# A linear-attention layer feeding a soft mixture of experts: the transfer of w behind the table load, the first k and r in halves, and idle products before the last expert

## The chip, the cores and the metric

The kernel runs on one core of one Trainium2 chip. The metric is the device time of one execution in microseconds. Five engines work side by side and wait for each other through semaphores: TensorE (PE in the profile; its weight loads are PEld), VectorE (DVE), ScalarE (ACT), GpSimd (POOL) and SyncE (SP), which here only issues transfers. The transfers themselves run on the core's 16 DMA engines.

## The reference

Two layers follow each other. The first is a recurrent attention over four batches, eight heads, 768 steps and a head size of 48:

```
for t in range(S):
    cur = u * k[t] (outer) v[t]
    y[t] = r[t] @ (state + cur)
    state = w[:, None] * state + k[t] (outer) v[t]
```

The second takes the 3072 by 384 result as x and mixes it softly into 32 slots, four for each of eight experts:

```
logits = x @ phi                       # 3072 x 32
d = softmax of logits over the rows;   slots = d.T @ x
out_e = relu(slots_e @ w1[e]) @ w2[e]  # w1: 384 x 1024, w2: 1024 x 384
c = softmax of logits over the slots;  result = c @ out
```

All inputs are float32. The sixteen expert matrices are by far the most of them.

## The kernel before

**Attention** is done in chunks of 128 steps, two chunks at a time, so that there are 12 units. For each, k and r are scaled by tables of powers of w (`tabs`, `tabl`), turned by TensorE, multiplied into a masked matrix and applied to v; a state runs from unit to unit. **The mixture** follows unit by unit: logits, the two softmaxes, the sums over the rows. When all rows are in, the experts run: H00 to H11 multiply the slots by w1, Q00 to Q13 multiply the hidden values by w2, and 24 products with `LexpT` (line 949) spread the result over the rows, are copied out of PSUM by ScalarE and VectorE in turn (lines 951 and 953) and are stored in eight transfers by SyncE (line 955).

**The order** is written out by hand. The string `ORDER` (lines 9 to 31) names every step, and `_Plan.run` (line 60) records the steps in that order, so that it is the program order on each engine. A step `Lk0` is the load of the first k; `Sk0` scales it on VectorE (line 427), `Tk0` turns it on TensorE. Words with F are idle products: `F19a_4` is four units of 256 columns, two of them to a product, of `mix` with the identity into a PSUM bank that nobody reads (line 861; the letter a names the bank `Ab`).

**The start** stands ahead of the plan, from line 208 on. ScalarE issues the transfer of w (line 211), broadcast over 128 partitions, and then loads its table of functions (line 212); it copies two permutations (lines 255 and 260), takes the logarithm of w (line 283), and from VectorE's products (line 281) it makes `tabs` (lines 287 and 288) and later `tabl` (line 397). TensorE meanwhile multiplies ones (line 219, `keep_warm`). SyncE's queue begins with k0, r0, u, v0, k1, r1. `load_f` (line 192) loads 32 rows of eight heads for one such step: 128 partitions, each holding two pieces (e = 0 and 1, the even and the odd heads) of 1536 bytes for the short steps (m even) and 3072 bytes for the long ones.

**The expert matrices** W0 to W15 are issued by GpSimd (lines 783 and 785), cast to bfloat16 on the way, into buffers that the attention has given back. The last one comes in two transfers: `W15a` holds seven of its eight rows of blocks, `W15` the eighth. Q12 (line 921) multiplies those seven, Q13 the eighth. Before Q12 stand Q11, which needs W14, and before that F19a_4.

Of the kernel before, what the change touches and what calls it, by code (L numbers as in the profile page):

```python
# [26 lines left out]
NB1 L3 AL2 ET2 YE11 AC1 ZT2 RM3 EE2 ZC3 EX3 SU2 F10a_3 X111 X110 XE111:ACT AL3 F11a_1 ET3 W15a ND1 XE110 EE3:ACT LB4  # L27
RM4 DP2 G1 DP3 AC2 EX4 G2 ET4 AL4 G3 G5 LC2 GS EE4 F12_3 DP4 AC3 ZT3 AC4 LX1 NM2 NB2 F13a_1 MG UN SU3 LC3 F14_6 H00
R00:DVE NM3 H01 R01 F15a_5 HT00 ND2 W15 HT01 HE00 F16a_1 Q00 HE01 Q01 H11 LE1:ACT R11 H10 LX2 R10:DVE NB3 LT4 ND3:ACT
SU4 F18a_2 HT11 HT10 HE10 HE11:ACT LC4 NM4 NB4 ND4:DVE Q10 LE2 LX3 LX4 LE3 F19a_4 Q11 Q12 LE4:ACT Q13  # L30
"""


# [12 lines left out]
class _Plan:  # L46
# [7 lines left out]
    def buf(self, pool):  # L54
        return _Buf(pool)

    def add(self, name, engs, fn, deps=(), bufs=()):
        self.by[name] = _Task(name, engs, fn, list(deps), list(bufs))
# [23 lines left out]
def kernel(  # L82
# [13 lines left out]
    B, H, S, D = r.shape  # L96
# [11 lines left out]
    R = 8  # L108
# [5 lines left out]
    CC = NS // U3  # L114
# [11 lines left out]
    def O(ins):  # L126
        return tc.keep_in_program_order(ins)

    pe, dve, act, pool, sp = nc.tensor, nc.vector, nc.scalar, nc.gpsimd, nc.sync
# [5 lines left out]
    RW = 2 * J * D  # L135
# [53 lines left out]

    def load_f(dst, a, m):
        b, lg = divmod(m, 2)
        jn = J if lg else JH
        O(sp.dma_start(out=dst[:, 0:2 * jn * D].rearrange("p (e x) -> p e x", e=2),  # L195
                       in_=a[b].rearrange("h (y j) d -> y h (j d)", j=jn)[lg * CC * R:lg * CC * R + 32]))

# [10 lines left out]
    for t in wu_t:  # L208
        O(dve.memset(t[:], 1.0))

    O(act.dma_start(out=w_f, in_=w.rearrange("(o q e) d -> o q (e d)", o=1, e=2).to_broadcast([C // nQ, nQ, P2])))
    O(act.preload_act_table_set("natural_log_exp_and_others"))

    warm = LexpT[:, 0:512]
    O(dve.memset(warm, 0.0))
# [128 lines left out]
    def consts_d():  # L344
# [5 lines left out]
    L = _Plan(dict(raw=raw, ks=ks_t, vj=vj_t, kn=kn_t, vn=vn_t, AT=AT_t, prs=pr_t[0:1], prl=pr_t[1:2], dv=dv_t,  # L350
                   **{f"{x}T": t for x, t in turned.items()},
                   S=S_t, Z=Z_t, x=x_t, zc=zc_t, Lc=Lc_t, Lcl=[Lc_t[0][:, NS - 2:]], Lsl=[Ls_t[0][:, NS - 2:]], Ls=Ls_t, E=E_t, ET=ET_t, T=T_t, A=[Ab], Y=[Yb], M=[Mb], **{f"xT{j}": [t] for j, t in enumerate(xT_t)}))
    buf, add = L.buf, L.add
# [17 lines left out]
    for m in range(NLD):  # L371
        for i, nm in enumerate("krv"):

            b, o = (kr["k", m][0], RH) if nm == "r" and m % 2 == 0 else (buf("raw"), 0)
            kr[nm, m] = b, o
            add(f"L{nm}{m}", "SP", (lambda b, o, a, m: lambda t: load_f(b.inst[:, o:RW], a, m))(b, o, (k, r, v)[i], m), bufs=[b])

    def load_phi(t):
        O(sp.dma_start(out=phi_f, in_=moe_phi.rearrange("(p q) s -> p q s", q=nM)))
# [13 lines left out]
    for h, av_, x in (("a", argl, slice(0, JH + 1)), ("b", argm, slice(JH, J + 1))):  # L393
        add(f"AH{h}", "DVE", (lambda av_, x: lambda t: argv_part(av_, e17l[:, x]))(av_, x))
        for i in range(2):

            add(f"TB{i}{h}", "ACT", (lambda i, h, av_: lambda t: O(act.activation(  # L397
                out=tabl[i][:, :, JH:J] if h == "b" else tabl[i][:, :, 0:JH],
                in_=av_[:, :, 1 - i:JH + 1 - i], func=AF.Exp, scale=(-1.0, 1.0)[i])))(i, h, av_),
# [3 lines left out]
    for m in range(NLD):  # L403
        lg = m % 2
        pb = TT["p", m] = buf("pr" + "sl"[lg])
        for nm in "krv":
            dstT = TT[nm, m] = buf(nm + "sl"[lg] + "T")
            P = P2 if nm == "v" else 128
            for h in range(1 + lg):
# [11 lines left out]
                else:  # L421
                    i = "kr".index(nm)
# [42 lines left out]
    for n in range(NU):  # L465
# [4 lines left out]
        m = 2 * bt + (ui > 0)  # L470
# [50 lines left out]
        def f_su(t, Mf=Mf, kn=kn, vn=vn, Sold=Sold, pb=pb, n=n, NK=NK):  # L521
# [13 lines left out]
            bufs=[Mf, vn, pb_, kn] + ([Sold] if ui else []))  # L535
# [26 lines left out]
        def f_y(t, Yf=Yf, rT=rT, vn=vn, dvb=dvb, Sold=Sold, Smid=Smid, a=tuple(ATb), n=n):  # L562
# [18 lines left out]
            bufs=[Yf, rTb, vn, dvb, Smid, ATb[0], ATb[1]] + ([Sold] if ui else []))  # L581
# [213 lines left out]
    for n in range(2 * E):  # L795
        wat[n] = buf("raw")
        wat[n].left += 4
        bufs, deps = [wat[n]], []
# [6 lines left out]
    nm = nm_t[(NPC - 1) % 2]  # L805
# [14 lines left out]
        bufs=[SXb])  # L820
# [118 lines left out]
    i = 0  # L939
# [46 lines left out]
```

## Time and profile before

| what | us |
|---|---|
| time, median of 3 runs (lowest, highest) | 119.17 (118.89, 119.31) |
| the profiled execution's own time | 120.24 |
| its span, first to last instruction | 118.5 |
| outside the span | 1.7 |
| busy: PE, DVE, ACT, POOL | 98.0, 94.8, 86.6, 61.0 |
| mean granted TensorE clock | 0.962 |
| moved by DMA | 31.81 MB as written, 39.42 MB read from HBM |

The profiled execution is 1.07 us longer than the median of the runs, so differences are worked out within the profile and then taken from the median. In the timeline each line gives the start in us, the busy time, the engine, the line of the code, what is written from what is read, the count, and in brackets how long the engine had been idle and who ended that. In the table of windows each row gives the stretch, its length, each engine's busy time with the number of instructions, then the granted TensorE clock, the busy share of the 16 DMA engines and the GB/s that they wrote. A share a little over 1 comes from counting whole packets where they begin.

### The profile page before, as it was taken

How to read it: one execution, taken by the hardware profiler on the slowest of the kernel's cores; microseconds unless marked ns; L12 is line 12 of the kernel's file. 1: busy time of each engine (PE TensorE's matmuls, PEld its weight loads, DVE VectorE, ACT ScalarE, POOL GpSimd, SP SyncE). 2: the span in 40 equal slices, each digit the busy share in tenths (PEclk: the TensorE clock that was granted, in tenths of full speed). 3: DMA queues.
4: the chain of work that ended last, by engine and by line, in shares of the span. 5: the costliest groups of instructions: out<-in, count | busy, mean ns of one | idle time of the engine just before them, and what ended most of it. 6: DMA issues, size and time to landing. Idle time of an engine off the chain costs nothing.

```text
span 118.5 us, 3926 instructions
## 1 busy us (share of the span) xinstructions
PE 98.0 (83%) x1660; PEld 71.1 (60%) x1660; DVE 94.8 (80%) x180; ACT 86.6 (73%) x140; POOL 61.0 (52%) x79
## 2 busy tenths in 40 slices
PE   3997895999999999989999989999899985498000
PEld 0364674787888787867788878686453542254000
DVE  6899987898999999999999989999786274099100
ACT  5769894999999999989899799979644151269000
POOL 7605899999999989999999010002303000000000
PEclk9999999999999999999999999999999999869955
DMA  2999999999999999999999999999999995059994
GB/s 31 333 387 374 364 408 397 383 390 401 384 384 391 297 229 223 219 215 214 217 212 221 210 223 207 223 207 219 212 212 218 216 207 104 12 199 407 419 402 166
DMA packets 10441, 31.81 MB, mean 268 GB/s; under 512 B 1080, under 2 KB 4408, under 8 KB 10424
## 3 DMA queue, kind: packets, MB, share of 16 engines
q0 software_dynamic: 2448, 12.58, 51.8%
q1 hardware_dynamic: 7832, 18.93, 42.3%
q8 instruction: 13, 0.21, 0.7%
q10 hardware_dynamic: 144, 0.05, 0.2%
q14 instruction: 4, 0.03, 0.1%
HBM read 39.42 MB, written 4.72 MB: 373 GB/s over the span
## 4 chain that ended last, share of the span: by engine, by line
PE 32%; DMA 23%; POOL 15%; DVE 9%; ACT 6%; issue 4%; SPq 3%; DVEq 0%; ACTq 0%; POOLq 0%
DMA raw<-in_moe_w_dram 16%; POOL mix L427 12%; PE T L436 7%; DMA raw<-in_r_dram 7%; PE Ab L506 3%; DVE mix L953 2%; PE Yb L572 2%; SPq L195 2%; PE T L491 2%; PE Yb L567 2%; DVE AT_all L511 2%; ACT xT_all L359 2%; PE Yb L578 2%; PE T L481 2%; PE T L595 2%
## 5 line engine op out<-in xcount | busy, mean ns | idle before, releaser
L427 POOL TENSOR_TENSOR mix<-raw,tabl 128x768 bf16<-128x768 f32 x15 | 27.7, 1858 | 5.8 <-ACT tabl L397 5.4
L511 DVE TENSOR_TENSOR AT_all<-Ab,mask 128x1024 bf16<-128x1024 f32 x24 | 29.3, 1219 | 1.1 <-PE Ab L506 0.5
L359 ACT COPY mix<-T 128x1024 bf16<-128x1024 bf16 x19 | 19.1, 1021 | 3.9 <-PE T L436 2.3
L436 PEld LDWEIGHTS <-mix 128*128 128x128 bf16 x192 | 11.8, 99 | 2.3 <-DVE mix L427 0.7
L555 DVE TENSOR_TENSOR dv<-vn,Mb 128x768 bf16<-128x768 bf16 x12 | 11.4, 946 | 1.4 <-PE Mb L545 1.1
L427 POOL TENSOR_TENSOR mix<-raw,tabs 128x768 bf16<-128x768 f32 x6 | 10.8, 1815 | 0.0
L359 ACT COPY vT_all<-T 96x1024 bf16<-96x1024 bf16 x10 | 10.2, 1021 | 0.5 <-PE T L436 0.4
L506 PE MATMUL Ab<-mix 64*128 64x128 bf16 x192 | 9.5, 218 | 1.2 <-ACT mix L359 1.0
L359 ACT COPY xT_all<-T 128x768 bf16<-128x768 bf16 (+1 forms) x12 | 9.3, 784 | 1.3 <-PE T L595 1.3
L359 ACT CAST x<-Yb 128x768 bf16<-128x768 f32 x12 | 9.7, 808 | 0.0
L436 PE MATMUL T<-turnl,mix 128*128 128x128 bf16 x128 | 9.6, 219 | 0.1
L359 ACT COPY vn<-T 128x768 bf16<-128x768 bf16 x11 | 8.8, 814 | 0.0
L452 DVE TENSOR_TENSOR pr<-T,mix 128x1024 bf16<-128x1024 bf16 x12 | 8.0, 681 | 0.0
L712 POOL TENSOR_TENSOR Lc<-Ls,sm 128x192 bf16<-128x192 f32 x2 | 1.0, 516 | 13.5 <-ACT E L690 13.5
L506 PEld LDWEIGHTS <-mix 64*128 64x128 bf16 x192 | 5.8, 94 | 3.5 <-issue 0.7
L572 PEld LDWEIGHTS <-AT_all 128*128 128x128 bf16 x192 | 6.6, 96 | 1.6
L359 ACT COPY kn<-T 128x768 bf16<-128x768 bf16 (+1 forms) x10 | 7.2, 722 | 0.1
L418 POOL CAST vj<-raw 128x768 bf16<-128x768 f32 x8 | 6.7, 832 | 0.6 <-POOL phi_s L336 0.6
L436 PEld LDWEIGHTS <-vj 128*96 128x96 bf16 x96 | 6.2, 123 | 1.2 <-issue 0.2
L572 PE MATMUL Yb<-vn,AT_all 128*128 128x48 bf16 x192 | 6.8, 183 | 0.0
L539 DVE TENSOR_TENSOR Z<-Mb,wT 128x384 bf16<-128x384 f32 x12 | 6.6, 553 | 0.1
L481 PE MATMUL T<-ident,mix 128*128 128x128 bf16 x80 | 6.1, 219 | 0.2
(187 smaller groups left out, 237.8 us busy)
## 6 DMA issues: line engine op xcount, KB each, us to landing
raw<-in_moe_w_dram POOLq DMA_DIRECT2D x13, 768.0 KB, 14.4
raw<-in_k_dram SPq DMA_DIRECT2D x4, 768.0 KB, 12.2
raw<-in_r_dram SPq DMA_DIRECT2D x4, 768.0 KB, 12.2
raw<-in_v_dram SPq DMA_DIRECT2D x4, 768.0 KB, 12.2
out_dram<-mix SPq DMA_DIRECT2D x3, 768.0 KB, 4.6
raw<-in_k_dram SPq DMA_DIRECT2D x4, 384.0 KB, 10.9
raw<-in_r_dram SPq DMA_DIRECT2D x4, 384.0 KB, 10.6
raw<-in_v_dram SPq DMA_DIRECT2D x4, 384.0 KB, 10.8
```

The costliest lines, as they stand in the source:

```text
L195: O(sp.dma_start(out=dst[:, 0:2 * jn * D].rearrange("p (e x) -> p e x", e=2), in_=a[b].rearrange("h (y j) d -> y h (j d)", j=jn)[lg * CC * ...
L359: O(act.copy(dst, src))
L418: O(act.copy(o, i_) if t.eng == "ACT" else pool.tensor_copy(o, i_))
L427: O(eng.tensor_mul(src.inst.rearrange("p (j e s) -> p e j s", j=JH, e=2)[:, :, :, 0:D], rv(), tab))
L436: O(pe.transpose(Tb.inst[0:P, jj * 128:(jj + 1) * 128], sv[:, jj, :], (turn, turnl)[lg][:]))
L452: O(dve.tensor_mul(cv(pb), tv(), cv(kT)))
L481: O(pe.transpose(Tb.inst[:, x * 128:(x + 1) * 128], kT.inst[:, x, :], ident[:]))
L506: O(pe.matmul(Abf.inst[:, e, x * C:(x + 1) * C], kT.inst[s, g * nQ + x, :], rT.inst[s, g * nQ + x, :]))
L511: O(dve.tensor_mul(AT.inst[:], Abf.inst[:].rearrange("p e (g t) -> p e g t", g=nQ), mask[:, None, None, :].to_broadcast([128, 2, nQ, C])))
L539: O(dve.tensor_mul(Smid.inst[:], Mf.inst[:, 0:SW].rearrange("p (q d) -> p q d", q=nQ)[:, :, None, :].to_broadcast([128, nQ, 2, D]), wT[:, ...
L555: O(dve.tensor_mul(dvb.inst[:].rearrange("p g e d -> p (g e) d"), vn.inst[:].rearrange("p g e d -> p (g e) d"), Mf.inst[:, 448:448 + 2 * P ...
L572: O(pe.matmul(y[:, x // nQ, q * P2 + e * D:q * P2 + (e + 1) * D], a[x // nQ].inst[:, e, q, :], vn.inst[:, x, e, :], start=False, stop=(c = ...
```

## The change

Three edits. The table load of ScalarE is recorded ahead of the transfer of w, on the same engine. The loads of k0 and r0 become two transfers each, one for each e, which fill the same bytes; SyncE's queue so has two more transfers. And F20a_10, five products of 512 columns into the bank `Ab`, is put between Q11 and Q12. Nothing that is computed changes.

```
-... F19a_4 Q11 Q12 LE4:ACT Q13
+... F19a_4 Q11 F20a_10 Q12 LE4:ACT Q13

-    def load_f(dst, a, m):
+    def load_f(dst, a, m, halves=False):
         b, lg = divmod(m, 2)
         jn = J if lg else JH
+        if halves:
+            for e in range(2):
+                O(sp.dma_start(out=dst[:, e * jn * D:(e + 1) * jn * D],
+                               in_=a[b].rearrange("(q e) (y j) d -> e y q (j d)", e=2, j=jn)[e, lg * CC * R:lg * CC * R + 32]))
+            return

+    O(act.preload_act_table_set("natural_log_exp_and_others"))
     O(act.dma_start(out=w_f, in_=w.rearrange("(o q e) d -> o q (e d)", o=1, e=2).to_broadcast([C // nQ, nQ, P2])))
-    O(act.preload_act_table_set("natural_log_exp_and_others"))

-            add(f"L{nm}{m}", "SP", (lambda b, o, a, m: lambda t: load_f(b.inst[:, o:RW], a, m))(b, o, (k, r, v)[i], m), bufs=[b])
+            add(f"L{nm}{m}", "SP", (lambda b, o, a, m, hv: lambda t: load_f(b.inst[:, o:RW], a, m, hv))(b, o, (k, r, v)[i], m, m == 0 and i < 2), bufs=[b])
```

More of the change, by code (lines that the diff above doesn't have):

```diff
@@ L29 @@
 R00:DVE NM3 H01 R01 F15a_5 HT00 ND2 W15 HT01 HE00 F16a_1 Q00 HE01 Q01 H11 LE1:ACT R11 H10 LX2 R10:DVE NB3 LT4 ND3:ACT
-SU4 F18a_2 HT11 HT10 HE10 HE11:ACT LC4 NM4 NB4 ND4:DVE Q10 LE2 LX3 LX4 LE3 F19a_4 Q11 Q12 LE4:ACT Q13
+SU4 F18a_2 HT11 HT10 HE10 HE11:ACT LC4 NM4 NB4 ND4:DVE Q10 LE2 LX3 LX4 LE3 F19a_4 Q11 F20a_10 Q12 LE4:ACT Q13
 """
```

## The prediction

> **What bounds the kernel now.** I read the page's rows of slices, then the chain that ended last, then the timeline and narrow windows of the two ends.
>
> ```profile
> DMA  2999999999999999999999999999999995059994
> ```
>
> Each digit is 1/40 of the span (2.96 us). The DMA engines are full from the second slice to the 33rd, and again over the stores. So the time is: start of the DMA stream, its volume, the gap in slices 34 to 36, the stores. The chain names the end of the stream:
>
> ```profile
> 82.73 18.82 DMA raw<-in_moe_w_dram
> ...
> 101.60 0.51 PE Yb L921 x7
> ```
>
> W15a is issued at 82.73 and lands at 101.56; TensorE's last seven rows start on it. These 18.8 us are a queue: a full expert matrix writes 786 KB, which at the 215 GB/s of the stretch 60 to 90 takes 3.66 us, so five lay ahead of it. What engines do between 12 and 98 us is therefore covered, as long as the queue doesn't run dry. The two ends are left. First the front:
>
> ```profile
> 0.73 0.63 ACTq L211 DMA_DIRECT2D LexpT<-in_w_dram  x1
> 0.73 0.71 SPq L195 DMA_DIRECT2D raw<-in_k_dram  x1
> ...
> 1.39 1.28 ACT L212 ACT_TABLE_LOAD   x1 [1.39 <-PEq L970]
> ...
> 1.49 0.80 SPq L195 DMA_DIRECT2D raw<-in_r_dram  x1
> ...
> 2.91 0.60 SPq L195 DMA_DIRECT2D raw<-in_v_dram  x1
> ...
> 3.43 0.28 ACT L283 ACTIVATE LexpT<-LexpT 128x96 f32<-128x96 f32 x1
> ```
>
> ```profile
> 2.00:2.50 0.50, 0.48 (x2) 0.00 (x0) 0.47 (x3) 0.50 (x1) 0.43 (x3) 1.00 0.65 78
> 2.50:3.00 0.50, 0.00 (x0) 0.00 (x0) 0.50 (x4) 0.49 (x2) 0.50 (x5) 1.00 0.62 116
> 3.00:3.50 0.50, 0.34 (x3) 0.26 (x4) 0.50 (x4) 0.50 (x4) 0.50 (x4) 1.00 0.89 273
> 3.50:4.00 0.50, 0.50 (x4) 0.22 (x3) 0.27 (x2) 0.21 (x2) 0.50 (x1) 1.00 1.06 393
> ```
>
> No byte moves before 2 us, and the engines are full only from 3.5. Then the back:
>
> ```profile
> 98.91 0.51 PE L921 MATMUL Yb<-tabl,AT_all 128*32 128x384 bf16 x8
> 101.60 0.84 PE L921 MATMUL Yb<-raw,AT_all 128*32 128x384 bf16 x8 [2.17 <-DMA raw<-in_moe_w_dram]
> ```
>
> ```profile
> 102.00:102.50 0.50, 0.43 (x4) 0.14 (x1) 0.00 (x0) 0.03 (x1) 0.00 (x0) 1.00 0.00 0
> 102.50:103.00 0.50, 0.00 (x0) 0.01 (x1) 0.00 (x0) 0.45 (x1) 0.00 (x0) 0.60 0.00 0
> 103.00:103.50 0.50, 0.50 (x3) 0.44 (x3) 0.00 (x0) 0.14 (x1) 0.00 (x0) 0.50 0.12 33
> ...
> 106.00:106.50 0.50, 0.50 (x5) 0.38 (x4) 0.50 (x2) 0.42 (x2) 0.00 (x0) 0.98 1.06 406
> 106.50:107.00 0.50, 0.50 (x5) 0.46 (x4) 0.50 (x2) 0.50 (x3) 0.00 (x0) 1.00 0.74 292
> ```
>
> TensorE waits 2.17 us for W15a, computes 0.84, waits 0.57 for the copy `so`, and about 3.2 us after it ran out of work the granted clock halves, from 102.6 to 106.0. In that time the 24 output products run 0.32 us apart (starts 103.59, 103.91, 104.23); at full clock they run 0.16 apart (106.74, 106.90, 107.06). The first stores are fed by the slow ones: the DMA share climbs only to 0.83 in the window 105 to 106 and dips to 0.74 at 106.5.
>
> **Part 1, idle products (F20a_10).** Five products of 512 columns; line 861 does two in 0.49 us at full clock (82.92), so 5 x 0.22 = 1.1 us. They start behind Q11 at 99.42 and end at 100.5: beside the wait, 1.07 us before W15a lands. Their bank is next written by an output product, later on the same engine, so nobody waits for them. In the 3.4 us up to 102.60 TensorE was busy about 0.23 + 0.84 = 1.07 us (31%) and the clock fell; with 1.1 more it is 64%. The threshold isn't in the trace: 31% loses the clock, stretches of 85% and more keep it. I take it that 64% keeps it, from the side on which most of the stretch is work.
>
> What that is worth, by the third store (three row groups, issued 105.83). At full clock the products come 0.16 apart, and the copies become the limit: VectorE's start 0.47 apart in warm stretches (108.16, 108.62, 109.09). First copy of VectorE at 103.39 (now 103.52), its second 103.69, then 104.16 and 104.63, which ends at 105.18; the third store goes out at 105.27 instead of 105.83. The dip at 106.5 shows that the DMA engines were waiting for just this store, and afterwards they are full to the end, so its 0.56 us go straight to the end: **-0.55 us**, at most -0.65; 0 if the clock falls all the same.
>
> The Trainium skill, "TensorE: Matmul & The Clock Gate", section "Why this matters for your kernels", asks for no idle gap over about 3 us and puts the drop after one idle window. That speaks against this edit: the largest gap here is 2.17 us, so by that sentence the clock would hold without the products and the term would be 0. The trace differs (0.50 from 102.6 to 106.0), and the measurement decides; the 3.4 us of the dip agree with its window.
>
> **Part 2, halves.** Two more issues on SP. A half has 128 rows. The nearest rows: stores of 128 rows take 0.33 to 0.36 us on SP, the issue of w's 128 rows 0.63 on ACT, loads of 256 rows 0.60 undisturbed. Ends 0.33 and 0.63; I take 0.45, nearer to SP's own rows. With the 0.05 between issues and u's 0.53, v0 goes out at 0.73 + 4 x 0.50 + 0.58 = 3.31 instead of 2.91 (2.83 to 4.03 at the ends), and all issues behind it as much later, until the queue is full: from 8.73 on single issues last up to 2.5 us because they wait for room.
> First bytes: w's came 0.8 us after the end of its issue (2.16), k0's 0.96 after (2.40). A first half issued by 1.18 then moves at about 2.1, 0.3 us sooner than k0 does now. Does v0 come in time? k0 and r0 are 393 KB each, 1.04 us at 378 GB/s. Started 0.3 sooner they end near 4.7; v0, 1.6 us behind its issue, arrives at 4.9 (4.4 to 5.6). So the gain of 0.3 is kept on an engine that is behind the others, and lost by 0.2 on one that is ahead; and the end is set by the engine that is last (shares fall 0.81, 0.45, 0.25, 0.08 from 98 to 102, so most had long finished). I take **-0.2 us**, bounds -0.4 and +0.6.
>
> **Part 3, w behind the table.** Either ScalarE's sequencer sends the table load off and issues w at once (about 0.8), or it issues after the load, at 2.0. The only row is the other order: there the load began at 1.39, 0.03 us behind the issue, so an issue does hold the load up. Bounds for w's landing: +0.05 and +1.28 us over 3.43. Between them I take the first for the sum, as a transfer needs nothing of ScalarE's datapath. Its price is the same, though: 0, as long as the cover holds. With the late w, line 283 moves 1.28, the tables too; GpSimd's first product (10.33, waiting for ScalarE's line 397) starts at 11.61 and ends at 13.45, where now the second starts at 12.48, on r1's landing: +0.97 for everything behind it. The expert issues move too, but lie up to 18.8 us deep in the queue; the first has least room (issued 35.55, its bytes flow from 38.7, the loads ahead drain near 40.5). Q11 would end at 100.4, the idle products at 101.5, just under the landing of W15a.
> The Trainium skill, "Perfetto Trace Analysis", section "DVE / Act Engine Instruction", has the sequencer free again once an instruction is pushed to a wait queue, and in "DMA Instruction — HWDGE" the sequencer itself issues transfers: by it w would not be late. No run here shows that order yet.
>
> **Sum**: -0.55 - 0.2 + 0 = -0.75 us: 120.24 becomes 119.5 under the profiler, 119.17 becomes **118.4** (0.63% faster).
>
> **Rivals.**
> - *The clock falls all the same* (64% is not enough, or the products lie in the wrong stretch). For it: one stretch is all we see. Then only the front counts: 119.0.
> - *v0 starves the DMA engines*: issues of 0.63 us. For it: the issues of w, k0 and r0 all take 0.63 or more. The front costs +0.6 instead of -0.2: 119.2 with the clock held, 119.8 without. Against: SP's 128-row stores.
> - *Slower: late tables push the idle products onto the path.* w issued at 2.0 and landing as late as k0 does (4.1 us later instead of 2.7) comes 2.7 us late. GpSimd then loses 13.03 + 1.84 - 12.48 = 2.4; Q11 ends at 101.8, and the products delay Q12 to 102.9, 1.3 us behind the landing. Less 0.55 for the clock: 119.9. It begins at 1.07 us of delay, and outweighs the gains above from about 1.8.
>
> **How the numbers follow.** Forecast 0.56 (118.4, alone 118.0 to 118.8), clock falls 0.16 (119.0), starved 0.14 (119.2, a third of it 119.8), late tables 0.14 (119.9). About 0.3% (0.36 us) is what a measurement can tell from no change: faster means under 118.81, slower over 119.53. So faster 0.56, same 0.26 (clock falls, two thirds of starved), slower 0.18. Range 118.0 to 119.7: it leaves out the worst of the last two.
>
> **What would show it.** Right: granted clock 1.00 through 102 to 109 and output products 0.16 apart from the first; third store 0.5 us sooner behind `so`; SP's first issue under 0.5 us and first bytes near 2.1; the landing of W15a near 101.3; line 283 at about 3.5. Wrong: a clock of 0.5 behind the idle products; a share under 0.9 near 4.5 to 5.5; line 283 beyond 4.5, with [idle] before Q12 gone.

## The result and the profile after

The changed kernel takes **120.30 us** (median of 20 runs, 119.50 to 120.98); the kernel before took 119.53 us beside it (median of 20, 118.86 to 121.16). The ratio is 1.0066, 95% interval 1.0043 to 1.0090: **slower by 0.66%**, some 0.8 us. The forecast was 118.4 us and faster, so it had the wrong sign. The two profiled executions hide this, because the one of before (120.24 us, span 118.5) lay high among its runs and the one of after (119.82, span 118.0) low. Spans are therefore not compared below, only stretches inside them. Ratios leave out executions that ran slower as a whole, so a ratio can stand a little off that of the medians, and e6 and e16, whose profiled execution was of that kind, have no rates in the table of runs.

**The middle is as it was.** First the row of DMA shares on the page of after, a digit to 1/40 of the span, then the links of its chain that end the stream:

```profile
DMA  2899999999999999999999999999999998149994
```

```profile
83.43 18.39 DMA raw<-in_moe_w_dram
101.82 0.04 issue
101.86 0.83 PE Yb L927 x8
```

The engines are full from the second or third slice to the 33rd, and W15a again spends 18.4 us in the queue. Whatever volume is missing at the front is therefore paid near 101.86. It moved the wrong way: Q12 starts 0.26 later than before (101.60), where the forecast had it 0.3 sooner.

**The front** on SyncE's queue, from the timeline of after (start, busy time, engine, line):

```profile
0.73 1.27 SPq L198 DMA_DIRECT2D raw<-in_k_dram  x2
2.05 1.24 SPq L198 DMA_DIRECT2D raw<-in_r_dram  x2
3.33 0.53 SPq L387 DMA_DIRECT2D LexpT<-in_u_dram  x1
3.92 0.62 SPq L201 DMA_DIRECT2D raw<-in_v_dram  x1
```

A half costs 0.58 to 0.63 us to issue (the first two lines hold two each, with some 0.05 between them), as much as a whole transfer of 256 rows (v0, the last line, 0.62). So v0 goes out at 3.92 instead of 2.91. The windows of after, to be laid beside those of before in the prediction (the last three columns are granted clock, DMA share and GB/s):

```profile
2.00:2.50 0.50, 0.50 (x2) 0.00 (x1) 0.47 (x4) 0.49 (x3) 0.43 (x3) 1.00 0.53 58
2.50:3.00 0.50, 0.30 (x3) 0.30 (x4) 0.50 (x5) 0.35 (x2) 0.50 (x5) 1.00 0.90 316
3.00:3.50 0.50, 0.50 (x4) 0.23 (x3) 0.28 (x2) 0.00 (x0) 0.50 (x4) 1.00 1.12 350
3.50:4.00 0.50, 0.50 (x3) 0.22 (x2) 0.00 (x0) 0.19 (x1) 0.50 (x1) 1.00 1.04 234
4.00:4.50 0.50, 0.50 (x3) 0.15 (x1) 0.37 (x1) 0.09 (x1) 0.50 (x2) 1.00 0.83 184
...
5.50:6.00 0.50, 0.24 (x2) 0.00 (x0) 0.38 (x3) 0.50 (x2) 0.00 (x0) 1.00 0.50 111
```

In the last of these stretches before had the first row below; the second is its row for 5 to 8 us, and the one by itself that of after:

```profile
5.50:6.00 0.50, 0.50 (x2) 0.15 (x1) 0.50 (x1) 0.50 (x1) 0.00 (x0) 1.00 0.98 335
...
5.00:8.00 3.00, 3.00 (x22) 1.64 (x21) 2.89 (x6) 1.93 (x4) 0.00 (x0) 1.00 1.03 368
```

```profile
5.00:8.00 3.00, 1.85 (x17) 0.90 (x16) 2.85 (x7) 2.18 (x5) 0.00 (x0) 1.00 0.82 267
```

Three things are to be read here. The stream does start sooner (316 GB/s from 2.5 to 3, where before had 116). Then, at 3.5, the engines are occupied (share 1.04) but move only 234 GB/s where before moved 393: their packets of 1536 bytes take longer (0.11 us on the mean from 3.5 to 4.5, before 0.07). And by 5.5 to 6 half of their time is idle, share 0.50. Added up over stretches against before: 2 to 3.5 us +0.13 MB (242 against 156 GB/s), 3.5 to 5 us -0.20 MB (250 against 382), 5 to 8 us -0.30 MB (267 against 368). In the first 16 us after moves 4.63 MB, before 4.90. At the 390 GB/s that both reach later, the missing 0.27 MB are 0.7 us. In these two executions only 0.26 us of that are left where W15a lands.

**ScalarE** in after:

```profile
0.73 1.28 ACT L217 ACT_TABLE_LOAD   x1 [0.73 <-PEq L976]
0.76 0.65 ACTq L218 DMA_DIRECT2D LexpT<-in_w_dram  x1
...
3.81 0.28 ACT L289 ACTIVATE LexpT<-LexpT 128x96 f32<-128x96 f32 x1 [0.96 <-DMA LexpT<-in_w_dram]
```

w is issued at 0.76, beneath the table load that began at 0.73. That w lands 0.38 later than before comes from the halves, which now move ahead of it: with the same order on ScalarE and whole transfers (run e3_w), line 283 starts at 3.43 as before, and with the halves and the old order (run e1_halves) it starts at 4.04. From e3_w:

```profile
3.43 0.28 ACT L283 ACTIVATE LexpT<-LexpT 128x96 f32<-128x96 f32 x1 [0.58 <-DMA LexpT<-in_w_dram]
```

**The back** of after: TensorE, then windows, then SyncE's third store, and by itself that of before.

```profile
99.61 0.51 PE L927 MATMUL Yb<-tabl,AT_all 128*32 128x384 bf16 x8
100.05 1.25 PE L867 MATMUL Ab<-mix,ident 128*128 128x512 bf16 x5
101.86 0.81 PE L927 MATMUL Yb<-raw,AT_all 128*32 128x384 bf16 x8 [0.56 <-DMA raw<-in_moe_w_dram]
...
103.57 0.33 PE L955 MATMUL Mb<-so,LexpT 128*128 128x384 bf16 x1
103.73 0.33 PE L955 MATMUL Ab<-so,LexpT 128*128 128x384 bf16 x1
```

```profile
102.50:103.00 0.50, 0.18 (x1) 0.15 (x1) 0.00 (x0) 0.28 (x1) 0.00 (x0) 1.00 0.00 0
...
106.50:107.00 0.50, 0.50 (x4) 0.33 (x3) 0.50 (x2) 0.50 (x2) 0.00 (x0) 1.00 0.98 406
```

```profile
105.51 3.41 SPq L961 DMA_DIRECT2D out_dram<-mix  x4
```

```profile
105.83 3.61 SPq L955 DMA_DIRECT2D out_dram<-mix  x4
```

The granted clock stays at 1.00, output products start 0.16 apart, the third store goes out at 105.51 (105.83 before, although Q12 started 0.26 later), and the dip to 0.74 at 106.5 has become 0.98. In this execution the part did what was forecast.

### The profile page after: what moved, and what is told of

It reads as the page before. It is cut to its first block, busy times and chain, and to the rows that moved or that the text cites. A ratio compares the mean times of both kernels' runs of the same rounds, so it can differ in the third digit from the quotient of the medians.

```text
span 118.0 us, 3934 instructions
## 1 busy us (share of the span) xinstructions
PE 97.9 (83%) x1661; PEld 71.1 (60%) x1665; DVE 94.1 (80%) x180; ACT 86.9 (74%) x140; POOL 61.4 (52%) x79
## 4 chain that ended last, share of the span: by engine, by line
PE 37%; DMA 18%; ACT 14%; DVE 14%; issue 4%; POOL 4%; DVEq 0%; ACTq 0%; POOLq 0%
DMA raw<-in_moe_w_dram 16%; PE T L442 9%; PE Ab L512 4%; DVE mix L959 3%; PE Yb L578 3%; POOL mix L433 3%; DVE AT_all L517 3%; DMA LexpT<-in_w_dram 3%; PE Yb L573 3%; ACT tabl L403 3%; ACT mix L365 2%; PE Yb L584 2%; PE Mb L535 2%; PE Mb L538 2%; PE T L601 2%
## 5 line engine op out<-in xcount | busy, mean ns | idle before, releaser
L867 PE MATMUL Ab<-mix,ident 128*128 128x512 bf16 (+1 forms) x25 | 6.4, 346 | 0.1
```

Source lines behind the costliest of these rows:

```text
L867: O(pe.matmul(o[:, 0:256 * min(n, 2)], ident[:], mix[:, 0:256 * min(n, 2)], start=True, stop=True))
```

## The experiments

Two theories stood at the start. **S** (starving): the halves take longer to issue, v0 comes late and the DMA engines run dry. **H** (halves): the divided transfers are slower in themselves, wherever v0 stands. The table gathers all runs: the ratio to the kernel before on the same chip, where v0 was issued, the rate of the DMA engines in three stretches, and what they moved in the first 16 us.

| run | ratio [95%] | v0 issued, us | GB/s 2-3.5 | 3.5-5 | 5-8 | MB by 16 us |
|---|---|---|---|---|---|---|
| before | 1 | 2.91 | 156 | 382 | 368 | 4.90 |
| after | 1.0066 [1.0043, 1.0090] | 3.92 | 242 | 250 | 267 | 4.63 |
| e1_halves | 1.0056 [1.0021, 1.0091] | 3.92 | 216 | 307 | 280 | 4.52 |
| e2_idle | 1.0012 [0.9979, 1.0045] | 2.92 | 147 | 372 | 356 | 4.96 |
| e3_w | 1.0014 [0.9980, 1.0047] | 2.96 | 123 | 396 | 350 | 4.98 |
| e4_no_halves | 0.9979 [0.9949, 1.0008] | 2.96 | 115 | 394 | 348 | 4.97 |
| e5_quarters | 1.0329 [1.0266, 1.0392] | 6.70 | 146 | 151 | 131 | 3.57 |
| e6_small | 1.0023 [0.9978, 1.0067] | 3.58 | - | - | - | - |
| e7_u_act | 1.0032 [0.9993, 1.0070] | 2.39 | 120 | 370 | 275 | 4.73 |
| e8_halves_u_act | 1.0058 [1.0009, 1.0107] | 3.34 | 230 | 268 | 262 | 4.55 |
| e9_halves_u_late | 1.0113 [1.0072, 1.0153] | 3.35 | 234 | 260 | 299 | 4.54 |
| e10_u_late | 1.0057 [1.0023, 1.0090] | 2.37 | 115 | 375 | 294 | 4.79 |
| e11_k0_halves | 1.0070 [1.0031, 1.0109] | 3.28 | 234 | 271 | 300 | 4.70 |
| e12_two_idle | 1.0003 [0.9962, 1.0044] | 2.96 | 137 | 371 | 375 | 4.92 |
| e13_halves_act | 1.0048 [1.0009, 1.0087] | 2.95 | 224 | 248 | 299 | 4.55 |
| e14_u_after_v0 | 1.0005 [0.9980, 1.0031] | 2.39 | 138 | 371 | 365 | 4.99 |
| e15_dummy | 1.0034 [1.0004, 1.0064] | 2.96 | 129 | 384 | 374 | 4.94 |
| e16_u_after_v0_two_idle | 1.0012 [0.9975, 1.0050] | 2.37 | - | - | - | - |
| e17_row_halves | 1.0100 [1.0066, 1.0133] | 4.20 | 183 | 259 | 262 | 4.37 |
| e18_k1_halves | 1.0040 [1.0007, 1.0074] | 2.97 | 146 | 388 | 338 | 4.78 |

The MB are those of one execution, the ratios those of many, and so the two agree only roughly. Still, 0.39 MB are 1 us of the stream, or 0.84%: e5 lacks 1.33 MB, which would be 3.4 us, and lost 3.9.

### The three edits one by one

**e1_halves** is the kernel before with the halves alone; **e2_idle** has `F20a_10` alone, **e3_w** the order on ScalarE alone; **e4_no_halves** is the changed kernel without the halves:

```
-  ... (k, r, v)[i], m, m == 0 and i < 2), bufs=[b])
+  ... (k, r, v)[i], m, False), bufs=[b])
```

> The halves of k0 and r0 alone, w and the products as before. Theory S (starved start): four issues of 0.62 us push v0's issue from 2.91 to about 3.9 us, the DMA share falls to 0.5 to 0.7 near 5 to 6 us, some 0.6 to 1.0 us of transfer are lost and the stream of expert matrices ends that much later: +0.6 to +1.0 us. Theory L (late tables and idle products on the path): the halves cost nothing, -0.3 to +0.3 us.

> The five idle products before Q12 alone. Both theories: the granted clock stays at 1.00 to 109 us and the output products come 0.16 us apart. Theory S: -0.2 to -0.55 us, less if many executions of the kernel before keep their clock anyway. Theory L: nothing delays TensorE here, since w is as early as before, so also -0.2 to -0.5 us.

> The table load ahead of w's transfer alone. Both theories: the issue of w starts about 0.03 us behind the start of the load, not behind its end, and line 283 (now 283 too) moves by less than 0.4 us. Theory S: within 0.3 us of before. Theory L: w lands later and all of the attention behind it by 0.3 to 0.7 us, but without the products there is room for it: within 0.3 us too.

> The changed kernel with k0 and r0 in one transfer each again. Theory S: the share near 5 to 6 us is back at 0.95 and more, and the time is that of the kernel before less the gain of the clock: -0.2 to -0.6 us against before. Theory L: w's delay and the products are still there, so the loss is too: +0.4 to +0.9 us against before.

The halves alone lose 0.56%, and taking them out of the changed kernel brings it from 1.0066 to 0.9979. So they carry the whole loss, 0.7 to 1.0 us. The new order of w alone does nothing that can be told from no change. With the idle products alone the clock held in the profiled execution, as one row of e2's windows shows (granted clock third from the end); the row below it is the same stretch of before, with 0.51:

```profile
102.50:106.00 3.50, 2.93 (x16) 2.11 (x16) 2.27 (x6) 2.74 (x7) 0.00 (x0) 1.00 0.27 96
```

```profile
102.50:106.00 3.50, 3.00 (x11) 1.78 (x12) 2.28 (x5) 2.21 (x5) 0.00 (x0) 0.51 0.31 114
```

From the start of Q12 to the end of the span, the twelve profiled kernels with idle products that held the clock there take 16.1 to 16.5 us (mean 16.3), and four without them (before, e1, e3, e11) 16.7 to 16.9 (mean 16.8): a gain of 0.4 us. That all of it comes from the clock isn't shown: e5, described below, kept its clock without such products and took 16.7. In the times of e2 the gain isn't seen, and its interval leaves room for 0.25 us at most. Q12 itself starts anywhere from 101.26 to 101.96 in kernels with a whole front (before, e2, e3, e4, e12), and that scatter is as large as the gain.

The granted clock of the other executions shows more. A fall of 3.41 us to 0.50 takes 0.014 off the mean clock of an execution, and the seven profiles that lost the clock between 102 and 105 us have a mean of 0.960 to 0.968 (before 0.962), since the idle end of the execution takes another 0.017 to 0.026 in them. Of the 128 executions of before that the ratios of e1 to e18 rest on, 59 have 0.970 or more, where hardly any room is left for such a fall; of the 136 executions of the twelve kernels with five products, 71 do. So the kernel before keeps its clock by itself in a good part of its executions, and its profiled one was not of them.

### More and smaller issues

**e5_quarters** gives k0 and r0 four transfers each of 64 rows; **e6_small** keeps them whole and puts two extra loads of 1.5 KB ahead of v0.

```
+            for e in range(2):
+                for p in range(2):
+                    O(sp.dma_start(out=dst[64 * p:64 * p + 64, e * jn * D:(e + 1) * jn * D], ...
...
+        for j in range(2):
+            O(sp.dma_start(out=spare[:, j, :], in_=u.rearrange("(q e) d -> q (e d)", e=2)))
```

> k0 and r0 in four transfers each of 64 rows, w and the products as before. Theory S (SP's issue time starves the DMA engines): an issue stays near 0.6 us however few rows it has, v0 goes out near 6.3 us, the DMA share falls below 0.6 from about 3 to 7 us, and the time is 2.0 to 3.3 us over before, three times the halves' loss or more. Theory H (each smaller transfer costs something of its own on the DMA engines, the queue time doesn't matter): twice the halves' loss, +1.0 to +1.5 us.

> The kernel before, with k0 and r0 whole, but u loaded three times, twice into a tile that nobody reads: two more issues of 0.53 us and 3 KB ahead of v0. Theory S: v0 goes out near 4.07 us instead of 2.91, the share dips near 5 to 6 us as with the halves, +0.4 to +0.9 us. Theory H: no transfer of k or r is smaller, so within 0.3 us of before.

e5 lost far more than either theory gave it, 3.9 us. Its timeline, and the window 4 to 5 us:

```profile
0.73 2.80 SPq L199 DMA_DIRECT2D raw<-in_k_dram  x4
3.58 2.51 SPq L199 DMA_DIRECT2D raw<-in_r_dram  x4
```

```profile
4.00:5.00 1.00, 1.00 (x4) 0.33 (x3) 0.99 (x3) 0.63 (x2) 0.96 (x4) 1.00 0.57 146
```

The issue of a quarter takes 0.59 to 0.78 us too, 0.66 on the mean of the eight with the steps between them. It carries 98 KB (64 rows of 1536 bytes), so SyncE feeds the engines 98 KB in each 0.66 us, 149 GB/s, and they move 146. The issue rate is the rate of the stream. The same sum for halves is 197 KB in 0.66 us, 298 GB/s, still under the 390 that the engines can move; for a whole k0 it is 393 KB in 0.66, about 600. This is S in a sharper form. e6 moved v0 to 3.58 and its interval holds both no loss and 0.7%: it decides nothing.

### Bringing v0 back

If a late v0 were all, v0 early again should mend the halves. **e8_halves_u_act** and **e7_u_act** (without halves) issue u on ScalarE's queue behind w; **e9_halves_u_late** and **e10_u_late** (without halves) put u behind k1:

```
+    O(act.dma_start(out=u_f[0:nQ], in_=u.rearrange("(q e) d -> q (e d)", e=2)))   (e7, e8)
-CB0 Lk0 Sk0 Lr0 Tk0 Sr0 LU Lv0 Ek0:ACT VC0:ACT Lk1 AHa
+CB0 Lk0 Sk0 Lr0 Tk0 Sr0 Lv0 Ek0:ACT VC0:ACT Lk1 LU AHa                             (e9, e10)
```

> The changed kernel without the halves, and u issued on ScalarE's queue behind w, beneath the table load, instead of on SP's. Theory S: v0 goes out at about 2.35 instead of 2.96, no dip of the share; -0.3 to -0.7 us against before, as e4_no_halves or up to 0.2 us better. Theory H: as e4_no_halves, -0.2 to -0.5 us.

> The changed kernel with its halves, and u on ScalarE's queue. Theory S: v0 goes out near 3.37 instead of 3.92, the dip near 5 to 6 us is smaller, and the time lies between the kernel before and the changed one, -0.2 to +0.4 us against before. Theory H: the halves cost the same as in the changed kernel, +0.5 to +0.8 us.

> The changed kernel with its halves, and u behind k1 on SP's own queue. Theory S: v0 goes out near 3.34 us instead of 3.92, r1 and all that follows as in the changed kernel; the stretch from 5 to 7 us moves more than the changed kernel's 393 KB, the time is 0.2 to 0.5 us below the changed kernel's. Theory H (the halves cost by themselves): as the changed kernel, +0.4 to +0.8 us against before.

> The changed kernel without the halves, and u behind k1 on SP's queue: v0 near 2.35 us, as in e7_u_act, but nothing added to ScalarE's queue. If an early v0 helps or does nothing (theory S): -0.2 to -0.6 us against before, as e4_no_halves, and some 5.0 MB moved by 16 us. If e7_u_act was slow because v0 came early: +0.2 to +0.5 us and 4.8 MB by 16 us, as there.

**e11_k0_halves** halves k0 alone (`i < 1`). **e13_halves_act** issues the second halves on ScalarE's queue, beneath the table load, with a 1.5 KB load on SyncE to hold v0 in its old place:

```
+    for a_, o in ((k, 0), (r, RH)):
+        O(act.dma_start(out=raw[0][:, o + JH * D:o + 2 * JH * D], ...[1, 0:32]))
```

> Only k0 in halves, r0 whole, w and the products as before: one more issue. Theory S: v0 near 3.4 us, the engines lose about half of what both halves lose, +0.1 to +0.5 us. Theory H: half too, +0.2 to +0.4 us; the two are told apart by where the bytes are missing: under S only behind v0's late issue (after 5 us), under H from 2.5 us on.

> The changed kernel with k0 and r0 in the same halves, but the second half of each issued on ScalarE's queue beneath the table load, and one small transfer of 1.5 KB on SP's queue, so that v0 goes out near 3.0 us as without halves. Theory S (SP's issue time, v0 too late): the idle time of the DMA engines between 5 and 8 us, 0.56 us per engine in the changed kernel, falls to 0.1 or less, and the time to -0.3 to +0.2 us against before. Theory H (the halves as such): idle time and loss stay, +0.5 to +0.9 us.

S doesn't survive these as the whole cause. From e9 and from e13, the issue of v0 and the stretch 5 to 8:

```profile
3.35 0.62 SPq L201 DMA_DIRECT2D raw<-in_v_dram  x1
```

```profile
5.00:8.00 3.00, 2.32 (x17) 0.94 (x16) 2.85 (x7) 2.18 (x5) 0.00 (x0) 1.00 0.88 299
```

```profile
2.95 0.63 SPq L201 DMA_DIRECT2D raw<-in_v_dram  x1
```

```profile
5.00:8.00 3.00, 3.00 (x14) 1.33 (x12) 2.16 (x6) 1.77 (x5) 0.00 (x0) 1.00 0.96 299
```

In e13 v0 goes out as early as in the kernel with whole transfers (e4, 2.96), k1 too (3.65 against 3.60), and the engines still move 299 GB/s from 5 to 8 us where that one moves 348. It isn't a clean repair: ahead of r1 SyncE waited 1.0 us for a transfer of r, so that r1 went out at 5.32 (e4 4.26, after 5.24). But with a share of 0.96 the engines had work. With shares of 0.88 and 0.96 at the same 299 GB/s, e9 loses more by idle engines and e13 more by slow packets. e9 should have gained on after by S and lost more (1.0113). Halving k0 alone (e11, 1.0070) loses as much as halving both (e1, 1.0056), where both theories had half.

### Losses without halves

e7 and e10 have no halves and come out slower anyway (e7's interval just holds no change), which neither theory had foreseen. In both, v0 and k1 are issued 0.6 us sooner than in e4. **e14_u_after_v0** puts u just behind v0 (`Lv0 LU`), so that v0 is early and k1 isn't; **e15_dummy** is e10 with a 1.5 KB load in u's old place, so that both are back.

> The changed kernel without halves, u just behind v0: v0 near 2.37 us, k1 and all behind it where e4_no_halves has them (3.6, 4.3). If an early v0 is what cost e10_u_late 0.7 us: the same here, +0.4 to +0.8 us, idle 0.25 us or more between 5 and 8 us. If it was k1's or r1's place: as e4_no_halves, -0.5 to 0.

> e10_u_late with another transfer of 1.5 KB (of w, into a tile that nobody reads) in u's old place: v0 near 2.96 us again. If the issue time of v0 decides: as e4_no_halves, -0.5 to 0 us against before, idle under 0.1 us between 5 and 8 us. If u's own transfer or its late place decides: as e10_u_late, +0.4 to +0.8 us.

From the timelines of e10 and of e14, the issues of v0 and of k1:

```profile
2.37 0.61 SPq L201 DMA_DIRECT2D raw<-in_v_dram  x1
3.02 0.61 SPq L201 DMA_DIRECT2D raw<-in_k_dram  x1
```

```profile
2.39 0.61 SPq L201 DMA_DIRECT2D raw<-in_v_dram  x1
...
3.63 0.60 SPq L201 DMA_DIRECT2D raw<-in_k_dram  x1
```

e10 moves 294 GB/s from 5 to 8 us, e14 365. An early v0 is harmless; it is k1, at 3.02 against 3.63, that goes with the missing rate. In time a late u is a rival. e15 has v0 and k1 in place, u at 4.26 and the rate back (374), and still comes out at 1.0034; e7, with an early k1 and no late u, at 1.0032; e10, with both, at 1.0057. The intervals overlap, so how the loss of e10 divides between the two isn't settled.

### The number of issues or the cut

**e17_row_halves** cuts k0 and r0 by rows instead of heads (64 partitions with both pieces); **e18_k1_halves** leaves k0 and r0 whole and cuts k1 and r1 by heads, where a half carries 393 KB.

```
+            for p in range(2):
+                O(sp.dma_start(out=dst[64 * p:64 * p + 64, 0:2 * jn * D].rearrange("p (e x) -> p e x", e=2), ...
...
+  ... (k, r, v)[i], m, m == 1 and i < 2), bufs=[b])                                    (e18)
```

> The changed kernel, but the two transfers of k0 and of r0 are split by rows (64 partitions with both pieces of 1536 bytes) instead of by heads (128 partitions with one piece). If the number of issues and bytes per issue is what costs (192 KB for each 0.66 us of issue is 298 GB/s, under the 390 GB/s that the DMA engines move), the loss stays: ratio 1.003 to 1.010, 5 to 8 us at 260 to 300 GB/s. If the split by heads costs (which rows each transfer reads, which engines get them), the loss goes: ratio 0.998 to 1.002, 5 to 8 us at 350 GB/s or more.

> The kernel with idle products and w behind the table load, k0 and r0 whole, but k1 and r1 in two transfers each, split by heads. A half of these holds 384 KB for some 0.65 us of issue (about 600 GB/s, more than the engines move), and v0 is issued at 2.96 as before. If the issue rate of the small halves is the cause, nothing is lost: ratio 0.996 to 1.002, 5 to 8 us at 345 GB/s or more. If the split by heads costs by itself, the loss is there, from 5 us on: ratio 1.003 to 1.010.

The cut by rows loses as much or more, so the choice of heads isn't the cause there; two more issues of 197 KB are common to both cuts. e18 speaks against the issue rate as the whole cause. Its ratio is 1.0040 where e4 has 0.9979, in the range that was expected if the cut itself costs; its rate from 5 to 8 is 338, 10 GB/s under e4's, and from 8 to 12 it is 352 where e4 has 409 and before 368. So dividing k1 and r1 costs too, later and less, though a half of this size feeds the engines at about 600 GB/s. Whether the two issues or the cut by heads do it there, no run tells.

### How many idle products

**e12_two_idle** is e4 with `F20a_4`, two products; **e16_u_after_v0_two_idle** is e14 with the same.

> The changed kernel without the halves and with two idle products of 512 columns before Q12 instead of five: 0.45 us of work more in the 3.4 us ahead of the drop, some 45% instead of 31 or 64%. If the limit for keeping the clock lies above 45%, the granted clock falls to 0.5 near 102.6 and the output products come 0.32 us apart; if below, it stays at 1.00.

> The kernel with u behind v0, but with two idle products instead of five. There Q12 followed the last of the five idle products at once (101.06, no idle time ahead of it), so the five set its start. If the landing of W15a is earlier than that, two products (0.65 us shorter) let Q12 start up to 0.5 us sooner, and the clock holds as it did with two products before: ratio 0.994 to 1.000. If W15a lands at 101.0 all the same, the time stays: ratio 0.998 to 1.003.

e12 held the clock at 1.00 to the end of its output products. e16 came out at 1.0012 [0.9975, 1.0050], so a shorter train of products brings nothing here. In its profiled execution, the longest of its twelve (121.29 us), Q12 waited 1.90 us, and from 103.1 the clock was 0.50, two products or not. e17 lost the clock with five products, from 104.67 on, when Q12 came at 102.80; e5 kept it without any, though Q12 waited 1.89 us. So the products neither hold it always nor are always needed.

## Why the prediction was wrong

**Volume and queue: right.** What the front loses, the end shows in the times. e5 is the clearest case: 1.33 MB missing by 16 us, 3.9 us on the time.

**Part 1, idle products: right in the profile, mis-sized in the times.** Clock, 0.16 us between output products and the missing dip at 106.5 came as described, and the third store came 3.65 us behind the start of Q12 instead of 4.23, 0.58 us sooner where 0.56 was forecast. What failed is the worth: "its 0.56 us go straight to the end", but 0.4 of them arrive there in the profiles. And the term was worked out from one profiled execution, which had lost the clock, and taken off a median of executions of which a good part keep it (59 of 128, by the clock above). e2's time, +0.14 us [-0.25, +0.54], leaves little of it; e4's, -0.25 us [-0.6, +0.1], fits a small gain and none.

That 64% of busy time would suffice was a guess, and 85% was not the nearest row that held: from 18.41 to 21.82 us before was busy 58% of the time at a clock of 1.00. The share doesn't decide by itself. In the profiles whose clock fell behind Q11 (before, e1, e3, e6, e11, e16, e17), TensorE had been busy 23 to 49% of the 3.41 us ahead of the fall (0.80 us in e11, 1.06 in before, 1.66 in e1); but e5, e8, e2 and e12 kept it through stretches of 3.41 us with 28, 43, 44 and 48%. Eleven of the twelve kernels with five products held it, one of the two with two, and one of the six without.

In each of the twenty profiles all changes of the clock lie whole multiples of 3.41 us apart (before: up at 7.03, down at 102.60, up at 106.02, down at 112.84), so where the idle stretch lies on that grid matters, and no edit here sets that. No clean limit comes out on the grid either: e8 kept its clock over a step with 53%, e9 lost it (at 13.55) behind one with 57%. The Trainium skill, "TensorE: Matmul & The Clock Gate", section "What's actually happening", has the clock judged over a free-running window of 3.4 us. Before, e1 and e3 agree, with dips of 3.4 us; and e17 agrees that the fall needn't follow a gap at once, since it came 0.49 us after TensorE had taken up work again (104.18).

**Part 3, w: right.** w went out at 0.76, beneath the table load that began at 0.73; e3's line 283 starts at 3.43; alone the new order makes no difference that can be told (1.0014 [0.9980, 1.0047]). The rule of the Trainium skill, "Perfetto Trace Analysis", section "DVE / Act Engine Instruction", that the sequencer is free once an instruction has been pushed to a queue, holds for this order, and the rival of late tables falls with it.

**Part 2, halves: wrong, and this decided the sign.** Forecast -0.2 us, measured +0.7 to +1.0. Three links of the step failed.

- *The issue.* "I take 0.45, nearer to SP's own rows": it is 0.58 to 0.63, with the step to the next some 0.65. Those rows were stores. The nearer rows were the loads, and they had shown 0.60 to 0.63 for w's 128 rows and for v0's 256 alike, so that there an issue's price didn't go by its rows. v0 came out at 3.92, near the late end of the bound (4.03).
- *The rate.* "k0 and r0 are 393 KB each, 1.04 us at 378 GB/s" took the full rate for transfers that are cut in two. A half of 197 KB in 0.66 us of issue is fed at 298 GB/s, and r0's packets were slow: 234 and 184 GB/s in the windows from 3.5 to 4.5. The 0.13 MB that the earlier start gained were gone by 5 us.
- *The bound.* "+0.6" priced only the wait for v0. The stretch 5 to 8 us lost 0.30 MB, 0.8 us, and e13 loses 0.15 to 0.2 MB there (299 GB/s against e4's 348 and before's 368) even with v0 and k1 on time.

The rival that came nearest, v0 starving the engines, had the issue right but not the price: with the clock held it made 119.2, no change, where the measurement gives +0.8 us. And a late v0 is only part of the cause.

The sum with the measured terms: between -0.4 (profiles) and +0.1 us (e2's time) for the products, 0 for w, +0.7 to +1.0 for the halves, so +0.3 to +1.1, around the measured +0.8 [0.5, 1.1]. Of the 1.9 us between 118.4 and 120.30, 0.36 are the base: before came out at 119.53, not 119.17.

**What stays open.** Dividing the first transfers is what costs: two more issues, with 197 KB each, lose 0.7 to 1.2 us (after, e1, e17), six more 3.9. The feed rate accounts for e5's rate and for part of what after loses. Why the engines still lag from 5 to 8 us when v0 and k1 are on time (e13, 299 GB/s), why one halved tensor costs as much as two (e11), why halves that are large enough cost as well (e18), and why the rate is missing without any halves when k1 goes out at 3.02 instead of 3.63 (e7, e10), isn't settled. The packets of after, sorted into 16 chains by their times, show some nine or ten of the engines idle for 0.4 to 1.4 us each from 5.0 to 5.4 on, and single packets of 1536 bytes, most of which take 0.065 us, that take longer: five take 0.3 to 0.4 us between 2.1 and 2.4, nine 0.3 to 0.7 between 3.6 and 4.3, eleven 0.3 to 0.9 between 5.3 and 6.6. Before has nine as slow between 2.4 and 3.1, when the stream is not yet running, one at 4.0 and five between 5.0 and 5.8. Whether these slow packets put the engines out of step and so cause the rest was not tried.

No run beats the kernel before beyond doubt. The best is e4, the change without its halves, at 0.9979 [0.9949, 1.0008].

## What to carry to other kernels

Cost an issue by rows of the same direction and queue, and divide its bytes by its time: a transfer that carries less than the stream moves in one issue slowed a stream here that had no queue yet (e5: 146 GB/s), however soon its first byte came. Where DMA bounds the kernel, compare the megabytes moved by a fixed time, in the profiles of both; that showed the loss where two spans of single executions hid it. Undo each part of a change alone: here one part carried the whole loss, and another did in the profile what was forecast and brought no time that can be told. And ask of a gain that is read from one profiled execution how many executions are like it; the mean granted clock of the others answered that here.

## What the runs showed of the hardware

- A load's issue on SyncE took 0.58 to 0.63 us for 128 rows, 0.60 to 0.65 for v0's 256 rows (0.70 to 0.84 for k0 and r0, the first two, when whole), 0.59 to 0.82 for 64 partitions (e5, e17), and 0.49 to 0.55 for four rows of 384 bytes; such a small load right behind another took 0.27 to 0.30 (e6, e13).
- The order of the first issues matters with the same bytes: u just behind v0 gave 1.0005 [0.9980, 1.0031] (e14), u one place further 1.0057 [1.0023, 1.0090] (e10), some 0.6 us apart.
- A second queue was no way out: with the second halves on ScalarE's queue the loss stayed (1.0048, e13), and its half of r0 landed 5.1 us after its issue, while the half of r0 on SyncE's took 3.9.
- The granted clock changed only on a grid of 3.41 us in each profile. A wait of 1.89 us for W15a left it at 1.00 in e5, one of 1.39 us took it to 0.50 in e3.
